# Four state scans on separate buffers, merged complex products, tables that start per base, shorter masks and a third parked query block in a fused attention and state-space kernel

## The chip, the cores and the metric

The kernel runs on one core of a Trainium2 chip. The metric is the device time of one launch in microseconds (us). Engines are named as in the profile: PE (TensorE matmul), PEld (its weight loads), DVE (VectorE), ACT (ScalarE), POOL (GpSimd), SP (SyncE, which issues nearly all DMAs).

## The reference

For x of shape 2048 x 512 in bf16, two branches are mixed by a gate:

```
g = sigmoid(sum(x * gate_w))                    # one number per row
a = softmax(q k^T / 4) v  for 32 heads of 16, q,k,v = x wqkv;   a = a wo
K[d,l] = Re( sum_n C[d,n] exp(dt[d] A[d,n] l) dt[d] B[d,n] )    # d < 512, n < 128, l < 2048
b = causal convolution of x with K along the rows, + x * Dskip
out = g * a + (1 - g) * b
```

Attention needs 32 x 2048 x 2048 exponentials. The convolution is done without an FFT, as a chunked state-space model: 32 chunks of 64 rows, a table of powers of the complex mode exp(dt A), states that are carried from chunk to chunk (the scan), and two small matmuls per chunk.

## The kernel before, in words

**Order of the work.** The kernel is written by a planner. Every instruction is an object `O` with an engine, the buffers it reads and writes, and a planned cost; `Prog.put` derives semaphore waits from them, also between two DVE instructions that depend on each other. Work is kept as threads (Python generators) with a priority; a smaller number goes first. `Sched.run` (line 363) takes, per exponential tile, the first thread in order of priority whose next instruction can start at once, and otherwise the least late one. A thread can wait for a flag (`("AFTER", name)`), for a tile number (`("Q", t)`) or for the one shared PSUM bank (`("LOCK", "MB")`); `landed` (line 326) gives the bank only when the planned landing of the transfers that its matmuls read lies 0.5 us back. The finished order is then fixed in each engine's instruction stream.

**Exponentials.** The scores are cut in 2048 slices of 512 columns, three to a tile; tiles go through two PSUM buffers SC. ACT takes the exponential of a tile in one instruction (line 755). From tile 380 on, `dchoose` (line 795) may give one slice of a tile to DVE, which makes it with integer and polynomial steps: line 767 for one slice, then four operations for a pair of slices (lines 787 to 791). Such slices use three PV matmuls each in place of one. `dchoose` returns without a choice when any DVE instruction of a thread with priority over 2.6 is ready, or when DVE is planned to be behind by more than a limit (4.6 or 5.5 us). Exponentials wait in rings: ET and EX, then EL (11 tiles, from tile 380) and EM (14 tiles, from tile 540). A block of 64 slices ends with a norm (lines 870 to 880).

**PE upkeep.** `lack` (line 246) counts planned PE activity in a window of 3.413 us; below NEED = 7.6 units the planner adds matmuls on a zero tile `wm`. Every matmul has an activity credit `u`, for example 0.05 for the gate's one-column matmuls.

**State-space half.** `params` (priority 10) computes the mode, its powers L1 to L48 and MU (the 64th) by `cmul` (line 904: four DVE operations, two of them 1024 wide in fp32) and one reciprocal (line 977). `bases` (11) makes four bases B16 of a quarter of the channels (128) each; `table` (9) makes eight pairs of blocks PT from them, after `base3` (line 1034). Each of the 16 blocks goes out to DRAM, comes back transposed as Qt, and meets the input blocks X2 in PE (`sstage`, line 1099: four PSUM evictions Sst a block); the chunk states go out and come back transposed into SG (`sload`, line 1124; three buffers for four quarters, so quarter 3 waits for `yq0`). `scan` (line 1142, priority 12) runs the quarters one after the other: 30 steps a quarter, each of five DVE operations on 128 channels, real and imaginary part: product with the real part of MU (s2), product with the imaginary part (s3), s2 plus SG, cast of the previous state into SG, and the sum into the state G. `ystage` (7.5) then makes 32 output units (line 1195), from Py and Tt loads, SG and X2; `yread`, `combine` and `outs` end the work.

**Start.** 14 one-column DVE operations (lines 661 to 669) make the two head masks; ACT first computes dt, then copies two parts of xT.

Of the kernel before, what the change touches and what calls it, by code (L numbers as in the profile page):

```python
# [6 lines left out]
FP32 = mybir.dt.float32  # L7
# [15 lines left out]
RS = 144  # L23
# [8 lines left out]
RINGS = ((24, "ET", NE), (380, "EL", 11), (540, "EM", 14))  # L32
DWS = ((380, 540 - 4, "DPL", "DCL", 4, 4.6), (540, 9999, "DPM", "DCM", 7, 5.5))
NEED = 7.6
# [3 lines left out]
SOLO = 1.0  # L38
ORDER = """
L8^ g1^ Q3^ VV^ VE ET D48 L4 EL CimT Dp^ fo^ OT^ nwi^ EX^ Qt^ Kst^ Q2^ Dpb Wv^ OnT2^ sgn u1^ X20^ sb_^ X23 gp^ Yl piota idf^ OnTp0  # L40
BimT Tt B161 Qp2^ L48^ SG0^ PT0 Q1^ B162 pt1 X22 SG1 OnT3^ BreT^ AreT ba^ cb^ MU SG2 OnT1 PT1 u4 L2 B163 g B160 Py^ dt^ wm L32 s3
an ON^ KT DPM ldt^ OnTp1^ xT^ ge^ AimT D16 Wk^ wrb^ X21^ tt2^ Sst hpi^ ft1^ Wq L16 ft2 zr tt1^ e2 idb^ EM VC^ x0n^ OnT0 Rz Q0 DPL
Yst^ u2 bn^ FP D32 DCM L1 CreT ea VL^ Wo Qp3^ msk s2^ DCL^ Qm^ gwT^ pt2 u3^ G zi
# [250 lines left out]
class Sched:  # L294
# [31 lines left out]
    def landed(self, ks):  # L326
        now = self.p.free["PE"] - .5
        return all(self.p.te[d] <= now for b, sl, *_ in (ks[0] if ks else ()) for d in b.st[sl][0].items())
# [80 lines left out]
def declare(nc, es):  # L409
# [9 lines left out]
    for k in (2, 3):  # L419
        sb(f"Qp{k}", 4 * 512)  # L420
# [65 lines left out]

    sb("SG0", 33 * 2 * RS)
    sb("SG1", 33 * 2 * RS)
    sb("SG2", 33 * 2 * RS)
    sb("G", 4 * 128, FP32)  # L490
    for n in ("s2", "s3"):
        sb(n, 2 * 128, FP32)

    for k in range(4):
        sb(f"X2{k}", 32 * 64)

# [11 lines left out]
    for n, free in (("ptd", NBLK * P * 2 * CB * T), ("sd", D * NCH * 2 * P),  # L508
                    ("kpd", NBLK * P * 8 * P), ("xrd", S * D), ("ytd", D * S), ("qd", 2 * P * 2048), ("od", 2 * P * S)):
# [66 lines left out]
def record(p, B, ins):  # L576
# [67 lines left out]
    for a in range(4):  # L644
# [9 lines left out]
        pool(lambda g: g.iota(pio(0, [[1, 1]]), [[0, 1]], base=0, channel_multiplier=1,  # L654
# [6 lines left out]
        dv(lambda v: v.memset(pio(1, [[1, 1]]), 0.0), [], [(pio, 1)], 1))  # L661
    for k in range(1, 8):
        put(dv(lambda v, k=k: v.scalar_tensor_tensor(pio(1 + k % 2, [[1, 1]]), pio(0, [[1, 1]]), 16.0 * k, pio(1 + (k - 1) % 2, [[1, 1]]),
                                                     ALU.is_ge, ALU.add), [(pio, 0), (pio, 1 + (k - 1) % 2)], [(pio, 1 + k % 2)], 1))
    put(dv(lambda v: v.memset(msk(0, [[1, 2]]), 0.0), [], [(msk, 0)], 1))
    for k in range(4):
# [939 lines left out]
```

## Time and profile before

| what | value |
|---|---|
| median of 6 runs (lowest, highest) | 881.92 us (877.23, 887.2) |
| the profiled execution, its span | 884.15 us, 882.4 us |
| mean granted PE clock | 0.986 |
| busy: PE, DVE, ACT | 786.5, 839.9, 859.6 us |
| exponential slices by DVE | 160 of 2048 |
| first exponential on ACT; end of the last | 13.3 us; 872.7 us |
| scan steps | 120, from 310 to 574 us |
| bytes by DMA | 96.5 MB |

A busy engine is not by itself the bound: the page gives averages over stages that are limited by different things, so the prediction reads busy time by stage, and the groups of instructions with their mean time. [...] two neighbours on DVE overlap by some 0.08 us, so what an instruction costs is read from the distance of starts in the timeline.

### The profile page before, as it was taken

The numbers are of one execution on the slowest core, as the hardware profiler recorded it, in microseconds if no ns is written. First come the engines' busy times: TensorE is split into PE (matmuls) and PEld (weight loads), VectorE is DVE, ScalarE is ACT, GpSimd is POOL, SyncE is SP. The second block draws the span as 40 slices with busy tenths as digits, with TensorE's granted clock in tenths as the row PEclk, the third lists the DMA queues.
The fourth block names the chain that finished last, engine by engine and source line by source line (L and its number), as shares of the span: only waits on it lengthen the run. The fifth ranks groups of instructions, "written<-read, shape, count | busy, mean of one in ns | idle before, by whom it ended". The sixth has DMA issues, their size and how long they took to land.

```text
span 882.4 us, 18472 instructions
## 1 busy us (share of the span) xinstructions
PE 786.5 (89%) x7566; PEld 248.3 (28%) x7566; DVE 839.9 (95%) x1802; ACT 859.6 (97%) x693; POOL 9.7 (1%) x18
## 2 busy tenths in 40 slices
PE   8988889998888888889899999999998998888887
PEld 3222222222222222222333334332332222222222
DVE  7999999999999999999999999999999999999992
ACT  7999999999999999999999999999999999999996
POOL 2000000000000000000000000000000000000000
PEclk9999999999999999998998899999999999999999
DMA  8410010006799999998866865545301100000000
GB/s 202 103 25 1 1 49 1 1 1 176 225 318 272 266 305 216 213 194 204 188 167 138 190 146 130 133 106 132 95 16 58 37 25 13 1 1 1 1 1 25
DMA packets 228564, 96.50 MB, mean 109 GB/s; under 512 B 192000, under 2 KB 215168, under 8 KB 226432
## 3 DMA queue, kind: packets, MB, share of 16 engines
q1 hardware_dynamic: 227280, 94.54, 43.8%
q8 instruction: 60, 0.98, 0.4%
q10 hardware_dynamic: 1200, 0.79, 0.4%
q14 instruction: 24, 0.20, 0.1%
HBM read 30.02 MB, written 37.75 MB: 77 GB/s over the span
## 4 chain that ended last, share of the span: by engine, by line
ACT 55%; DVE 35%; PE 6%; DMA 2%; issue 2%; ACTq 0%; DVEq 0%; SPq 0%
ACT ET L755 33%; ACT EL L755 15%; DVE EM L767 5%; DVE DCM L884 4%; ACT EM L755 4%; DVE ft L884 3%; ACT EX L755 3%; DVE tt L884 3%; PE OA L590 3%; DVE s L884 3%; PE SC L590 2%; DVE Sst L1113 2%; DVE EL L767 2%; DVE PT L884 1%; DVE DCL L884 1%
## 5 line engine op out<-in xcount | busy, mean ns | idle before, releaser
L755 ACT ACTIVATE ET<-SC 128x1536 bf16<-128x1536 f32 x362 | 488.5, 1655 | 5.6 <-PE SC L590 5.5
L590 PE MATMUL SC<-Qm,KT 32*128 32x512 bf16 x2048 | 269.9, 388 | 73.6 <-ACT ET L755 29.7
L590 PE MATMUL OA<-wm 128*128 128x512 bf16 x592 | 189.2, 395 | 1.8 <-DVE wm L656 1.0
L755 ACT ACTIVATE EL<-SC 128x1536 bf16<-128x1536 f32 (+1 forms) x160 | 183.7, 1351 | 0.6 <-PE SC L590 0.4
L590 PEld LDWEIGHTS SC<-Qm,KT 32*128 32x128 bf16 x2048 | 67.8, 91 | 335.3 <-ACT ET L755 162.2
L755 ACT ACTIVATE EM<-SC 128x1024 bf16<-128x1024 f32 (+1 forms) x143 | 157.1, 1246 | 1.7 <-PE SC L590 1.4
L590 PE MATMUL OA<-ET,VE 128*32 128x512 bf16 x1086 | 109.5, 398 | 0.7 <-DVE OT L872 0.7
L884 DVE TENSOR_TENSOR s<-G,MU 128x256 f32<-128x256 f32 x240 | 92.7, 419 | 3.3
L884 DVE TENSOR_TENSOR tt<-B,D 128x1024 bf16<-128x1024 bf16 x96 | 62.6, 682 | 0.5
L590 PEld LDWEIGHTS OA<-wm 128*128 128x128 bf16 x592 | 40.4, 98 | 76.5 <-issue 65.4
L767 DVE TENSOR_SCALAR EM<-SC 128x512 int16<-128x512 f32 x84 | 55.7, 679 | 0.5 <-PE SC L590 0.5
L767 DVE TENSOR_SCALAR EL<-SC 128x512 int16<-128x512 f32 x76 | 51.1, 682 | 1.8 <-PE SC L590 1.7
L884 DVE TENSOR_TENSOR G<-s,s 128x256 f32<-128x256 f32 x120 | 50.2, 418 | 0.1
L884 DVE TENSOR_TENSOR s<-s,SG 128x256 f32<-128x256 f32 x120 | 49.9, 416 | 0.0
L590 PE MATMUL OA<-EL,VE 128*32 128x512 bf16 x480 | 46.4, 389 | 0.0
L1113 DVE TENSOR_TENSOR Sst<-MB,sgn 128x512 bf16<-128x512 f32 x64 | 43.6, 682 | 1.9 <-PE MB L590 1.9
L590 PEld LDWEIGHTS OA<-ET,VE 128*32 128x32 bf16 x1086 | 27.6, 94 | 61.9 <-issue 59.7
L590 PE MATMUL OA<-EM,VE 128*32 128x512 bf16 x428 | 42.8, 390 | 0.1
L590 PE MATMUL MB<-Qt,X 64*32 64x256 bf16 x512 | 29.1, 303 | 9.5 <-DVE Sst L1113 5.8
L872 DVE STREAM_TRANSPOSE OT<-OA 128x512 f32<-128x512 f32 x32 | 22.7, 708 | 13.8 <-PE OA L590 13.8
L1155 DVE CAST SG<-G 128x256 bf16<-128x256 f32 x120 | 34.4, 287 | 0.1
L884 DVE TENSOR_TENSOR ft<-FP,L 128x1024 f32<-128x1024 f32 (+1 forms) x32 | 33.9, 1085 | 0.4
(163 smaller groups left out, 856.9 us busy)
## 6 DMA issues: line engine op xcount, KB each, us to landing
gm_ptd<-PT SPq DMA_DIRECT2D x16, 1024.0 KB, 6.2
Py<-gm_ptd SPq DMA_DIRECT2D x32, 512.0 KB, 4.6
gm_sd<-Sst SPq DMA_DIRECT2D x64, 128.0 KB, 2.8
gm_kpd<-Kst SPq DMA_DIRECT2D x16, 256.0 KB, 6.4
Tt<-gm_kpd SPq DMA_DIRECT2D x128, 32.0 KB, 3.6
gm_xrd<-in_A_x_dram SPq DMA_DIRECT2D x1, 2048.0 KB, 12.0
X<-gm_xrd SPq DMA_DIRECT2D x8, 256.0 KB, 5.2
gm_ytd<-Yst SPq DMA_DIRECT2D x32, 64.0 KB, 2.1
```

The source lines that it names most:

```text
L590: return O("PE", lambda t: t.matmul(out(), lhsT(), rhs(), start=start, stop=stop, skip_group_check=True, **kw), R, W, c, l, u)
L755: return ac(lambda a: a.activation(b(o, F), sc(0, F), AF.Exp, scale=LN2 / 128), [(sc, n, (t, n)) for n in ns], [et(t, n)[2] for n in ns], ...
L767: yield [dv(lambda v: v.tensor_scalar(b(o, [[1, 512]]).bitcast(I16), sc(512 * n, [[1, 512]]), -EOFF, EOFF, ALU.max, ALU.add), [(sc, n, (t, ...
L872: yield [dv(lambda v: v.transpose(OT(0, [[1, 512]]), OA(0, [[1, 512]])), [(OA, 0, b)], [(OT, 0, b)], 560)]
L884: return dv(lambda v: v.tensor_tensor(o(), a(), b_(), f), R, W, n, k)
L1113: yield [dv(lambda v, bank=bank: v.tensor_tensor(Sst(512 * bank, [[256, 2], [1, 256]]), MB(0, [[256, 2], [1, 256]]), sgn(0, [[0, 2], [1, 2 ...
L1155: return dv(lambda v: v.tensor_copy(sg(2 * RS * r, [[RS, 2], [1, 128]]), G(256 * (r % 2), V2)), [(G, r % 2)], [(sg, bl, (qr, 'G')) for bl ...
```

## The change

- The state scan becomes four threads (priority 12, 12.1, 12.2, 12.3), one for each quarter, each with its own SG, its own state G and its own products Gm. The two products of a step are one operation of 512 elements; MU is stored as imaginary part, real part, minus imaginary part for it.
- The loads of SG no longer wait for a freed buffer but for a tile number (172, 222, none, 300). Quarters 0 and 1 of X2 are loaded a second time into X2a and X2b for the y stage, after S13.
- Squares of complex numbers use `csq`, four operations of 512 elements. exp(-2 an) on ACT takes the place of a square and a reciprocal on DVE.
- `table` waits for the base that its pair of blocks needs (and one ahead), not for the last.
- `dchoose` ignores ready scan steps while the scan keeps to a straight line from its state at tile 380 to its end at tile 421. Ring EM has 13 tiles and starts at tile 548.
- The masks take three one-column operations. Query block 1 is stored and loaded back as blocks 2 and 3 are. One ACT copy of xT goes ahead of dt.
- `landed` asks for 2.5 us, NEED is 7.5, and the gate's matmuls have no activity credit. The order of placement in the on-chip memory is a new list.

```diff
-RINGS = ((24, "ET", NE), (380, "EL", 11), (540, "EM", 14))
-DWS = ((380, 540 - 4, "DPL", "DCL", 4, 4.6), (540, 9999, "DPM", "DCM", 7, 5.5))
-NEED = 7.6
+TL = 380
+TE = 548
+NL = 11
+NM = 13
+PEND1 = 4.6
+PEND2 = 5.5
+RINGS = ((24, "ET", NE), (TL, "EL", NL), (TE, "EM", NM))
+DWS = ((TL, TE - 4, "DPL", "DCL", 4, PEND1), (TE, 9999, "DPM", "DCM", 7, PEND2))
+NEED = 7.5
 WIN = 3.413
 HALF = .44
 TOL = .2
 SOLO = 1.0
+SGQ = (172, 222, 0, 300)
+SGP = 6
+SCN = 380, 421
...
     def landed(self, ks):
-        now = self.p.free["PE"] - .5
+        now = self.p.free["PE"] - 2.5
...
-    sb("SG0", 33 * 2 * RS)
-    sb("SG1", 33 * 2 * RS)
-    sb("SG2", 33 * 2 * RS)
-    sb("G", 4 * 128, FP32)
-    for n in ("s2", "s3"):
-        sb(n, 2 * 128, FP32)
+    for k, (a, b) in enumerate(PARTS):
+        sb(f"SG{k}", 33 * 2 * (128 * (b - a) + 16))
+    for k, (a, b) in enumerate(PARTS):
+        sb(f"G{k}", 512 * (b - a), FP32)
+        sb(f"Gm{k}", 512 * (b - a), FP32)
 
     for k in range(4):
+        sb(f"X2{k}", 32 * 64)
+    for k in "ab":
         sb(f"X2{k}", 32 * 64)
 
...
     put(dv(lambda v: v.memset(hpi(0, [[1, 1]]), HALF_PI), [], [(hpi, 0)], 1),
-        dv(lambda v: v.memset(pio(1, [[1, 1]]), 0.0), [], [(pio, 1)], 1))
-    for k in range(1, 8):
-        put(dv(lambda v, k=k: v.scalar_tensor_tensor(pio(1 + k % 2, [[1, 1]]), pio(0, [[1, 1]]), 16.0 * k, pio(1 + (k - 1) % 2, [[1, 1]]),
-                                                     ALU.is_ge, ALU.add), [(pio, 0), (pio, 1 + (k - 1) % 2)], [(pio, 1 + k % 2)], 1))
-    put(dv(lambda v: v.memset(msk(0, [[1, 2]]), 0.0), [], [(msk, 0)], 1))
-    for k in range(4):
-        put(dv(lambda v, k=k: v.scalar_tensor_tensor(msk(1, [[1, 1]]), pio(2, [[1, 1]]), 2.0 * k + 1, msk(1, [[1, 1]]),
-                                                     ALU.is_equal, ALU.add), [(pio, 2), (msk, 0)], [(msk, 0)], 1))
-    put(dv(lambda v: v.tensor_scalar(msk(0, [[1, 1]]), msk(1, [[1, 1]]), -1.0, 1.0, ALU.mult, ALU.add), [(msk, 0)], [(msk, 0)], 1))
+        dv(lambda v: v.tensor_scalar(pio(1, [[1, 1]]).bitcast(I32), pio(0, [[1, 1]]).bitcast(I32), 16, None, ALU.bitwise_and),
+           [(pio, 0)], [(pio, 1)], 1),
+        dv(lambda v: v.tensor_scalar(msk(1, [[1, 1]]), pio(1, [[1, 1]]).bitcast(I32), 1 / 16, None, ALU.mult), [(pio, 1)], [(msk, 0)], 1),
+        dv(lambda v: v.tensor_scalar(msk(0, [[1, 1]]), msk(1, [[1, 1]]), -1.0, 1.0, ALU.mult, ALU.add), [(msk, 0)], [(msk, 0)], 1))
...
-            if any(isinstance(x[3], list) and x[3][0].eng == "DVE" and (p.ready(x[3]) or 0) < end for x in sch.thr if x[0] > 2.6):
+            fore = scn[0] >= 120 - max(0, 120 - scn[1]) * (SCN[1] - t) / (SCN[1] - SCN[0])
+            if any(isinstance(x[3], list) and x[3][0].eng == "DVE" and (p.ready(x[3]) or 0) < end
+                   for x in sch.thr if x[0] > 2.6 and not (fore and x[0] >= 12)):
                 return
...
+
+    def csq(o, x, tk=("pt1", "pt2")):
+        o, x, t1, t2 = B[o], B[x], B[tk[0]], B[tk[1]]
+        k = int(o is B["MU"])
+        yield [tt(half(t1, 0), half(x, 0), half(x, 1), ALU.subtract, [(x, 0)], [(t1, 0)])]
+        yield [tt(half(t2, 0), half(x, 0), half(x, 1), ALU.add, [(x, 0)], [(t2, 0)])]
+        yield [dv(lambda v: v.scalar_tensor_tensor(o(D - D * k, [[1, D]]), x(0, [[1, D]]), 2.0, x(D, [[1, D]]), ALU.mult, ALU.mult),
+                  [(x, 0)], [(o, 0)], D)]
+        yield [tt(half(o, k), half(t1, 0), half(t2, 0), ALU.mult, [(t1, 0), (t2, 0)], [(o, 0)])]
+
+    def power(o, x, y):
+        return csq(o, x) if x == y else cmul(o, x, y)
...
         for o, x, y in (("L2", "L1", "L1"), ("L4", "L2", "L2"), ("L8", "L4", "L4")):
-            yield from cmul(o, x, y)
+            yield from power(o, x, y)
...
-        yield [tt(perm("u1"), nat("ea"), nat("ea"), ALU.mult, key("ea"), key("u1"))]
-        yield [dv(lambda v: v.reciprocal(B["e2"](0, [[1, D]]), B["u1"](0, [[1, D]])), key("u1"), key("e2"), 3050)]
+        yield [ac(lambda a: a.activation(B["e2"](0, PERM), B["an"](0, NAT), AF.Exp, scale=-2.0), key("an"), key("e2"), D)]
...
-        yield [dv(lambda v: v.tensor_scalar(MU(2 * D, [[1, D]]), MU(D, [[1, D]]), -1.0, None, ALU.mult), key("MU"), [(MU, 1)], D, 2)]
+        yield [dv(lambda v: v.tensor_scalar(MU(2 * D, [[1, D]]), MU(0, [[1, D]]), -1.0, None, ALU.mult), key("MU"), [(MU, 1)], D, 2)]
...
         yield ("AFTER", "projs")
         yield ("AFTER", "gate")
-        yield ("AFTER", "base3")
         t1, t2 = B["tt1"], B["tt2"]
         for pb in range(NBLK // 2):
             qr, blks = pb // 2, (2 * pb, 2 * pb + 1)
             PT = PTs[pb % 2]
+            yield ("AFTER", f"base{min((pb + 1) // 2, 3)}")
...
+    XY = [B["X2a"], B["X2b"], X2[2], X2[3]]
...
     def sload(blk):
-        qr, bl = divmod(blk, 4)
-        if qr == 3:
-            yield ("AFTER", "yq0")
-        elif qr == 1:
-            yield ("AFTER", "sgfree")
-            yield ("Q", p.q + 3)
-        sg = SG[qr % 3]
+        k, sg, rs, a = part(blk // 4)
+        bl = blk - 4 * a
+        yield ("Q", max(SGQ[k], p.q + 3))
         if bl == 0:
-            yield [pool(lambda g: g.memset(sg(0, [[1, 2 * RS]]), 0.0), [], [(sg, "z")], 256)]
-            if qr < 3:
-                yield [pool(lambda g: g.memset(sg(2 * RS + 128, [[RS, 64], [1, 16]]), 0.0), [], [(sg, "pad")], 1024)]
-        yield [dma("SP", lambda e: e.dma_start_transpose(sg(2 * RS + CB * bl, [[RS, 64], [1, CB]]),
+            yield [pool(lambda g: g.memset(sg(0, [[1, 2 * rs]]), 0.0), [], [(sg, "z")], 2 * rs)]
+        yield [dma("SP", lambda e: e.dma_start_transpose(sg(2 * rs + CB * bl, [[rs, 64], [1, CB]]),
                                                          sd.dram(CB * blk * 8192, [[8192, CB], [1, 8192]])),
-                   [(sd, (blk, i)) for i in range(4)], [(sg, bl, (qr, 'S'))], 6.3, 2.6)]
+                   [(sd, (blk, i)) for i in range(4)], [(sg, bl, (k, 'S'))], 6.3, 2.6)]
         sch.mark(f"sg{blk}")
...
-        def quarter(qr):
-            sg, d0 = SG[qr % 3], 128 * qr
...
+        def run(k):
+            G, Gm = B[f"G{k}"], B[f"Gm{k}"]
+            a, b = PARTS[k]
+            sg, rs, d0, w, nb = SG[k], 128 * (b - a) + 16, 128 * a, 128 * (b - a), 4 * (b - a)
+            V2 = [[w, 2], [1, w]]
+            ks = [(sg, bl, (k, 'S')) for bl in range(nb)]
...
             for r in range(2, NCH):
-                k, o = r % 2, 1 - r % 2
-                yield [tt(lambda o=o: s2(0, V2), lambda o=o: G(256 * o, V2), lambda: MU(d0, [[0, 2], [1, 128]]), ALU.mult,
-                          [(G, o), (MU, 0)], [(s2, 0)], 256)]
-                yield [tt(lambda: s3(0, V2), lambda o=o: G(256 * o + 128, [[-128, 2], [1, 128]]), lambda: MU(D + d0, [[D, 2], [1, 128]]), ALU.mult,
-                          [(G, o), (MU, 0), (MU, 1)], [(s3, 0)], 256)]
-                yield [tt(lambda: s2(0, V2), lambda: s2(0, V2), lambda r=r: sg(2 * RS * r, [[RS, 2], [1, 128]]), ALU.add,
-                          [(s2, 0)] + ks, [(s2, 0)], 256)]
+                o, i = r % 2, 1 - r % 2
+                yield [tt(lambda: Gm(0, [[2 * w, 2], [w, 2], [1, w]]), lambda i=i: G(2 * w * i + w, [[-w, 2], [0, 2], [1, w]]),
+                          lambda: MU(d0, [[D, 2], [D, 2], [1, w]]), ALU.mult, [(G, i), (MU, 0), (MU, 1)], [(Gm, 0), (Gm, 1)], 4 * w)]
+                yield [tt(lambda: Gm(0, V2), lambda: Gm(0, V2), lambda r=r: sg(2 * rs * r, [[rs, 2], [1, w]]), ALU.add,
+                          [(Gm, 0)] + ks, [(Gm, 0)], 2 * w)]
                 if r > 2:
                     yield [cast(r - 1)]
-                yield [tt(lambda k=k: G(256 * k, F), lambda: s2(0, F), lambda: s3(0, F), ALU.add, [(s2, 0), (s3, 0)], [(G, k)], 256)]
+                yield [tt(lambda o=o: G(2 * w * o, V2), lambda: Gm(0, V2), lambda: Gm(2 * w, V2), ALU.add, [(Gm, 0), (Gm, 1)], [(G, o)], 2 * w)]
+                scn[0] += b - a
+                if p.q <= SCN[0]:
+                    scn[1] = scn[0]
             yield [cast(NCH - 1, True)]
-            sch.mark(f"scan{qr}")
+            for qr in range(a, b):
+                sch.mark(f"scan{qr}")
 
         yield ("AFTER", "scanpar")
-        for qr in range(4):
-            yield from quarter(qr)
+        for k in range(len(PARTS)):
+            sch.add(run(k), 12 + .1 * k)
...
             yield ("AFTER", f"scan{qr}")
             yield ("AFTER", f"yl{u}")
+            while 1 not in XY[qr].st:
+                yield ("Q", p.q + 1)
             yield ("LOCK", "MB", [(Py, r)] + [(Tt, (r, par, a)) for par in range(2) for a in range(2)])
...
         for qr in range(4):
-            yield ("Q", 30) if qr == 0 else ("AFTER", f"S{4 * qr - 3}")
-            for par in range(2):
-                yield [dma("SP", lambda e, qr=qr, par=par: e.dma_start(X2[qr](0, [[64, 32], [1, 64]], 64 * par, 64),
-                                                                       B["xrd"].dram(64 * qr + 256 * par, [[32 * D, 64], [D, 32], [1, 64]])),
-                           [(B["xrd"], 0)], [(X2[qr], par)], 8, 1.9)]
+            yield ("Q", 30) if qr == 0 else ("AFTER", f"S{4 * qr - 2}")
+            yield from fetch(X2[qr], qr)
             sch.mark(f"ub{qr}")
+        yield ("AFTER", "S13")
+        for qr in range(2):
+            yield from fetch(XY[qr], qr)
...
-                      [xk(lt // 4, q4), (gwT, 0)], [(MB, 0, 'gate')], q4 == 0, q4 == 3, c=.06, l=.2, u=.05)
+                      [xk(lt // 4, q4), (gwT, 0)], [(MB, 0, 'gate')], q4 == 0, q4 == 3, c=.06, l=.2, u=0.0)
...
-        for c, q in ((2, 322), (3, 458)):
+        for c, q in ((1, 156), (2, 322), (3, 458)):
...
-    put(copy_dve(*cp[0]), copy_dve(*cp[2]))
+    put(copy_dve(*cp[0]), copy_dve(*cp[2]), copy_act(*cp[1]))
     put(O("ACT", lambda a: a.activation(B["dt"](0, [[1, D]]), B["ldt"](0, [[1, D]]), AF.Exp), key("ldt"), key("dt"), .55))
-    put(copy_act(*cp[1]), copy_act(*cp[3]))
+    put(copy_act(*cp[3]))
```

## The prediction

> **What bounds the kernel now.** I read the page first, then busy time by stage, then the groups with shapes kept apart, then the DVE timeline inside the scan. Engine totals:
>
> ```profile
> PE 786.5 (89%) x7566; PEld 248.3 (28%) x7566; DVE 839.9 (95%) x1802; ACT 859.6 (97%) x693; POOL 9.7 (1%) x18
> ```
>
> ACT is full, and DVE is full beside it. They share one pool of work: 2048 exponential slices of 512 columns, of which DVE took 160 (76 into EL, 84 into EM). So DVE time is worth something: what it does not spend on the state-space half, it can spend on exponentials. The stage table (us; PE, PEld, DVE, ACT busy with counts, then PE clock, DMA share, GB/s) and the same stretches for the DVE exponential, line 767, alone:
>
> ```profile
> 531.00:576.00 45.00, 43.61 (x620) 17.21 (x619) 42.99 (x131) 45.00 (x35) 0.00 (x0) 1.00 0.57 139
> 576.00:720.00 144.00, 131.49 (x1406) 42.74 (x1406) 142.06 (x291) 143.38 (x132) 0.00 (x0) 1.00 0.27 67
> 720.00:860.00 140.00, 120.84 (x1012) 34.11 (x1009) 139.40 (x280) 138.30 (x129) 0.00 (x0) 0.99 0.02 5
> ```
>
> ```profile
> 440.00:531.00 91.00, 0.00 (x0) 0.94 0.69 158
> 531.00:576.00 45.00, 0.69 (x1) 1.00 0.57 139
> 576.00:720.00 144.00, 52.44 (x78) 1.00 0.27 67
> 720.00:860.00 140.00, 53.70 (x81) 0.99 0.02 5
> ```
>
> No slice goes to DVE before 531 us, where tile 380 and ring EL begin, and one from 531 to 576: there DVE is busy with the rest of the scan. The last scan cast stands at 573.7 us; from then on 159 slices follow in 284 us. The scan itself, from the DVE timeline (start, duration; an "x2" covers two):
>
> ```profile
> 499.54 0.76 DVE L884 TENSOR_TENSOR s<-G,MU 128x256 f32<-128x256 f32 x2
> 500.21 0.42 DVE L884 TENSOR_TENSOR s<-s,SG 128x256 f32<-128x256 f32 x1
> 500.55 0.29 DVE L1155 CAST SG<-G 128x256 bf16<-128x256 f32 x1
> 500.75 0.42 DVE L884 TENSOR_TENSOR G<-s,s 128x256 f32<-128x256 f32 x1
> 501.20 0.76 DVE L884 TENSOR_TENSOR s<-G,MU 128x256 f32<-128x256 f32 x2
> ```
>
> One step recurs every 1.66 us (499.54 to 501.20). Independent 256-wide operations start 0.33 us apart and the cast takes 0.20, so five operations make 4 x 0.333 + 0.20 = 1.53; the other 0.12 to 0.13 is the next product waiting for the sum written just before it.
>
> Last, stretches of 4 us with a low PE clock:
>
> ```profile
> 408.00:412.00 4.00, 4.00 (x32) 0.84 (x24) 3.46 (x9) 2.96 (x3) 0.00 (x0) 0.56 0.62 117
> 412.00:416.00 4.00, 4.00 (x38) 1.07 (x35) 2.82 (x8) 3.17 (x4) 0.00 (x0) 0.58 1.21 294
> 480.00:484.00 4.00, 4.00 (x46) 1.27 (x38) 3.96 (x14) 2.96 (x3) 0.00 (x0) 0.52 0.60 121
> 484.00:488.00 4.00, 4.00 (x41) 1.12 (x40) 2.58 (x8) 3.37 (x3) 0.00 (x0) 0.50 1.15 269
> 488.00:492.00 4.00, 4.00 (x23) 0.86 (x22) 3.93 (x13) 2.97 (x3) 0.00 (x0) 0.70 0.95 168
> ```
>
> ACT loses 1.04 + 0.83 = 1.87 us at 408 to 416, where PE stood waiting for a Qt transfer (1.4 us in the waits), and 1.04 + 0.63 + 1.03 = 2.70 us at 480 to 492, inside the y stage. Two more dips, at 132 (the gate's 64 one-column matmuls) and 784 us, cost 0.29 and 0.88.
>
> [...] 419 ns at 256 elements, 682 to 688 at 512, 1218 at 1024, about 1.04 ns per element. [...] Here 0.333 us minus 267 ns gives 66 ns: that is what one instruction less is worth. [...]
>
> **The exchange rate.** From 720 to 860 us DVE is busy 139.4 us; six norms (0.64 + 0.15 + 0.34 + 0.27 + 0.31 = 1.71 us each by their starts) and four output evictions (0.67) take 13. So (139.4 - 13) / 81 = 1.56 us of DVE per slice. What a slice takes from ACT is the difference of two rows:
>
> ```profile
> L755 ACT ACTIVATE EM<-SC 128x1024 bf16<-128x1024 f32 x85 | 81.5, 1082 | 0.7 <-PE SC L590 0.6
> L755 ACT ACTIVATE EM<-SC 128x1536 bf16<-128x1536 f32 x58 | 81.1, 1488 | 1.0 <-PE SC L590 0.8
> ```
>
> 81.1/58 = 1.40 and 81.5/85 = 0.96, so 0.43 us. If DVE is freed by d and takes n slices more, the span falls by 0.43 n, and DVE loses that time too: d = (1.56 + 0.43) n. One us freed gives 0.50 slice and 0.216 us of span. By the same argument one us of ACT time removed or added changes the span by 1 - 0.216 = 0.78 us.
>
> **The change part by part.**
>
> *Merged scan product.* Two 256-wide products (2 x 0.333) become one of 512 (0.600, as the other 512-wide fp32 rows start): 0.067 x 120 steps = 8.0 us of DVE.
>
> *Interleaving.* A lone new step is 0.600 + 0.333 + 0.20 + 0.333 = 1.47, plus two exposed dependences of 0.12 (product to add, sum to next product; the cast still covers the third) = 1.71, worse than 1.66. With a second quarter on its own G and Gm every gap is filled: 1.47. Before, from 320 to 530 us, the listed DVE operations sum by starts to 195 of 210 us, idle stalls are some 5, so 10 us of gaps remain for 96 steps: 0.105 per step. Full cover is worth 0.105 x 120 = 12.6 us. Quarters have equal claims only by order: two alternate at a time, and quarter 0 starts alone from tile 172 (244 us), when tables fill its gaps. I take 12.6; bounds 0 and 14.
>
> *Squares.* The rows of a complex product and the reciprocal:
>
> ```profile
> L884 DVE TENSOR_TENSOR pt<-L 128x1024 f32<-128x1024 f32 x12 | 14.3, 1218 | 0.1
> ...
> L884 DVE TENSOR_TENSOR L<-pt,pt 128x512 f32<-128x512 f32 x12 | 8.1, 672 | 0.1
> ...
> L977 DVE RECIPROCAL e<-u 128x512 f32<-128x512 f32 x1 | 3.3, 3344 | 0.0
> ```
>
> Six squares lose two 1024-wide products (1.13 by starts) for two 512-wide ones: 2 x 0.53 = 1.07, and one exposed wait, 0.12: 1.19 x 6 = 7.1 us. L48, VL stay products.
>
> *Reciprocal.* 3.25 by starts, and the ea square 0.60: 3.85 us off DVE. ACT gets one 512-column exp; its like (ea, line 1404) lasts 0.64, by slope 0.43 to 0.5: ACT +0.5, span +0.4. No table load, since it is Exp amid Exp.
>
> *Tables per base.* The same instructions sooner: the table may start after base 0 instead of base 3 at 192 us, some 45 us earlier. DVE is 98% busy there anyway, so nothing falls on the path; the DMA phase (share 1.01 from 300 to 380) starts while the queue is idle, and bases fill the tables' 0.12 us gaps. Some 160 such gaps stand in bases and tables, partly filled now: worth 0 to 10, I take 3 us.
>
> *Exponentials beside the scan.* The choice of a slice no longer yields to a ready scan step once the scan keeps its pace. It removes the hole at the switch (DVE idle 2.0 us in 560 to 580). The freed time must find slices at tile 380: what the scan did after 531 us was 43 us of DVE, so up to about 43 us freed can be absorbed. Bound: beyond that DVE would idle before tile 380.
>
> *Landing margin 0.5 to 2.5 us, gate counted as no activity.* Both aim at dips above: ACT 1.87 + 0.29 = 2.16, span 1.7. Behind a wrongly early S matmul stood the score matmuls, hence ACT. The y dip (2.70) has another cause and stays. NEED 7.5 for 7.6 removes some warm matmuls; they lie in PE's slack, 14% from 720 on, so nothing gained; see the rival.
>
> *Three-operation masks, ACT copy first.* The masks ended at 6.0 us, ahead of x0n at 6.3: nothing. The copy fills ACT's wait for ldt; an started at 8.10 because DVE was busy, so dt 0.2 later is covered: within 0.2 either way.
>
> *DMAs and queues.* Added: one store and one load of Q1 (0.5 MB each), four X loads of 0.25 MB (one seen issue held SP for 3 us, another 0.5; 5.2 us to land), fewer POOL memsets. About 2 MB on 96.5. They pass on SP ahead of Py, Tt and Yst transfers; in 440 to 531 the DMA share is 0.69. The y stage now also waits for the new X buffers after S13; before, its 32 evictions ran from about 437 to 665 us and the first outputs went out at 700, the last exp at 872, so 100 us late would still be hidden.
>
> Sum: 8.0 + 12.6 + 7.1 + 3.85 + 3 + 2 = 36.5 us of DVE, so 18 slices (178) and 7.9 us of span; plus 0.4, minus 1.7: -9.2 us. The profiled execution was 884.15 us, its span 882.4: 873.2 and about 875. It lies 2.2 above the median of 881.92 (runs 877.23 to 887.2), so for the median I take 872.7.
>
> **The rivals.**
>
> *A wider gain.* The y dips go too (DMA spread out, later locks): 2.70 + 0.88 times 0.78 = 2.8; all base and table gaps fill: 7 us more DVE, 1.5. That gives 868.4. For: DMA shares of 0.6 to 1.15 stand in the stretches of the dips. Against: 784 us has no DMA.
>
> *The interleaving finds no partner.* Quarters gated by their loads (quarter 3 not before tile 300, about 417 us) run alone at 1.71: scan 120 x 0.05 = 6 us dearer instead of 20.6 cheaper. DVE freed 7.1 + 3.85 + 2 - 6 = 7, span 1.5; with +0.4 and -1.7 this is -2.8: 879. Against it: before, all 16 S blocks were done at 438 us, so two quarters should be there together.
>
> *The clock gives way: slower.* The plan holds PE activity just over NEED; [...] The four dips cost ACT 5.74 us, 1.43 each, 1.1 of span. Eight more dips eat the gain; sixteen make 891. [...] For: 1.3% less margin. Against: the dips seen had causes of their own (a wait, one-column matmuls), not a bare margin.
>
> **How the numbers follow.** First case 0.55 (own range 869 to 877), wider gain 0.22, no partner 0.14, clock 0.09. One per cent, about what a measurement of this kernel tells from none, is 873.1. The first case lies at that border, and most of what I left out (gaps in bases and tables) is gain: 0.35 of it counts as faster, 0.20 as same. Faster 0.35 + 0.22 = 0.57; same 0.20 + 0.14 = 0.34; slower 0.09. Range 865 to 881: it takes in the wider gain with some slices more, and the no-partner case.
>
> **What would show it.** Right: 170 to 186 slices at line 767's operation, some between 531 and 576; products of 128x512 at about 688 ns, 120 of them; steps of two quarters alternating with starts 0.33 and 0.60 apart; ACT busy 7 us less; no clock dip at 132 and 410. Wrong: DVE idle between 480 and 531 (nothing to do before tile 380), 160 slices again, new dips, or outputs after the last exp.

## The result, and the profile after

The changed kernel takes 880.2 us (median of 32 runs, 875.26 to 882.81) against 883.74 us for the kernel before on the same chips (67 runs): a ratio of 0.9956, 95% interval 0.9942 to 0.9969. That is 3.5 us less; 9.2 were forecast. The profiled execution has a span of 878.6 us (before 882.4). Its time, 880.42 us, is near the median; its mean clock, 0.982, is below the 0.9875 that the 32 runs have on average.

The line of engine totals of the page after, to set beside the first fence of the prediction:

```profile
PE 780.5 (89%) x7548; PEld 246.4 (28%) x7548; DVE 835.1 (95%) x1717; ACT 854.0 (97%) x694; POOL 6.4 (1%) x15
```

ACT is 5.6 us less busy. But span minus ACT busy, that is ACT's idle time, rose from 882.4 - 859.6 = 22.8 to 878.6 - 854.0 = 24.6 us. The slices on DVE (stage table of the DVE exponential, now line 774; columns us, DVE busy with count, clock, DMA share, GB/s):

```profile
440.00:531.00 91.00, 0.00 (x0) 1.00 0.60 148
531.00:576.00 45.00, 13.27 (x20) 1.00 0.56 127
576.00:720.00 144.00, 50.49 (x76) 1.00 0.21 50
720.00:860.00 140.00, 53.10 (x80) 0.99 0.02 5
```

176 slices instead of 160, and 20 of them where there was one: the freed DVE time was found and spent as the prediction said. The scan's and the tables' groups (out<-in, shapes, count, busy us, mean ns, idle before):

```profile
L893 DVE TENSOR_TENSOR Gm<-G,MU 128x512 f32<-128x512 f32 x120 | 80.9, 684 | 1.2
...
L893 DVE TENSOR_TENSOR Gm<-Gm,SG 128x256 f32<-128x256 f32 x120 | 49.3, 417 | 0.9
...
L893 DVE TENSOR_TENSOR pt<-L 128x512 f32<-128x512 f32 x12 | 7.8, 686 | 0.1
...
L998 ACT ACTIVATE e<-an 128x512 f32<-128x512 f32 x1 | 1.2, 1172 | 0.0
```

The 120 merged products last 684 ns, the squares' first operations 686 ns instead of 1218. The last row is the ACT exponential that took the reciprocal's place.

What went wrong shows in 4-us stretches with a low PE clock (us; PE, PEld, DVE, ACT, POOL busy; clock; DMA share; GB/s):

```profile
288.00:292.00 4.00, 4.00 (x25) 0.85 (x24) 3.71 (x8) 3.06 (x3) 0.00 (x0) 0.50 0.98 353
292.00:296.00 4.00, 4.00 (x32) 0.98 (x31) 2.39 (x6) 3.19 (x3) 0.00 (x0) 0.50 0.74 148
...
416.00:420.00 4.00, 0.42 (x8) 0.20 (x8) 1.37 (x3) 1.54 (x2) 0.00 (x0) 0.71 1.03 239
420.00:424.00 4.00, 4.00 (x33) 0.89 (x25) 3.13 (x8) 2.58 (x2) 0.00 (x0) 0.50 0.78 209
```

The dips of before at 132, 410 and 480 us are gone, but between 288 and 296 us ACT loses 0.94 + 0.81 us, and between 416 and 424 us 2.46 + 1.42. A third new dip stands at 372 to 380. The DVE timeline there (start, duration, [idle before <- releaser]) and the waits from 410 to 421 us (total, times, longest):

```profile
414.94 0.42 DVE L893 TENSOR_TENSOR G<-Gm 128x256 f32<-128x256 f32 x1
418.63 0.29 DVE L1174 CAST G<-SG 128x256 f32<-128x256 bf16 x1 [3.27 <-DMA SG<-gm_sd]
418.84 0.68 DVE L1135 TENSOR_TENSOR Sst<-MB,sgn 128x512 bf16<-128x512 f32 x1
```

```profile
PE MB L601 <- DVE Sst L1135: 4.0, 1, 4.0
ACT ET L762 <- PE SC L601: 3.3, 1, 3.3
DVE G L1174 <- DMA SG<-gm_sd: 3.3, 1, 3.3
```

Read them as a chain. DVE reached the first step of the third quarter's scan, the cast of its first state row (line 1174), at 415.4 us, and stood 3.27 us because the SG load had not landed. Queued behind it on DVE was an eviction of a state block (Sst, line 1135); PE needed its PSUM bank and stood 4.0 us; the score matmuls behind that on PE came late, so ACT stood 3.3 us. From 417.7 us the clock is 0.50 for 6.8 us (in the first dip for 13.6, from 284.6), and ACT loses a fifth to a third of its time there as well (0.81 to 1.42 us of 4). At 279 us the first quarter's cast waited 1.28 us in the same way. By the planner's own times the cast of the third quarter was due at 409.74 us and the load at 409.69: ordered with 0.05 us to spare; the four quarters of the change have 1.0, 1.0, 0.05 and 9.0 us. In the kernel before, by the same planner, a quarter's first cast came 1.0 us after its last load in the first quarter and 13 to 19 us after it in the others.

### The profile page after: what moved, and what is told of

Same layout as the page of the kernel before. It is cut to its first block, busy times and chain, and to the rows that moved or that the text cites. A ratio compares the mean times of both kernels' runs of the same rounds, so it can differ in the third digit from the quotient of the medians.

```text
span 878.6 us, 18380 instructions
## 1 busy us (share of the span) xinstructions
PE 780.5 (89%) x7548; PEld 246.4 (28%) x7548; DVE 835.1 (95%) x1717; ACT 854.0 (97%) x694; POOL 6.4 (1%) x15
## 4 chain that ended last, share of the span: by engine, by line
DVE 46%; ACT 43%; PE 6%; issue 2%; DMA 2%; ACTq 0%; DVEq 0%; SPq 0%
ACT ET L762 29%; DVE Gm L893 10%; ACT EL L762 9%; DVE EM L774 5%; DVE DCM L893 5%; DVE G L893 4%; DVE EL L774 3%; ACT EX L762 3%; PE OA L601 3%; DVE DCL L893 3%; PE SC L601 2%; DVE SG L1177 2%; ACT EM L762 2%; DVE Sst L1135 2%; PE MB L601 2%
## 5 line engine op out<-in xcount | busy, mean ns | idle before, releaser
L762 ACT ACTIVATE EL<-SC 128x1024 bf16<-128x1024 f32 (+1 forms) x168 | 186.4, 1287 | 0.9 <-PE SC L601 0.4
L601 PE MATMUL OA<-wm 128*128 128x512 bf16 x547 | 177.1, 397 | 1.8 <-DVE wm L667 1.0
L762 ACT ACTIVATE EM<-SC 128x1024 bf16<-128x1024 f32 (+1 forms) x135 | 147.9, 1262 | 0.3
L893 DVE TENSOR_TENSOR Gm<-G,MU 128x512 f32<-128x512 f32 x120 | 80.9, 684 | 1.2
L774 DVE TENSOR_SCALAR EL<-SC 128x512 int16<-128x512 f32 x96 | 63.8, 679 | 1.3 <-PE SC L601 1.2
L601 PEld LDWEIGHTS OA<-wm 128*128 128x128 bf16 x547 | 37.9, 98 | 73.0 <-issue 62.4
L774 DVE TENSOR_SCALAR EM<-SC 128x512 int16<-128x512 f32 x80 | 53.1, 678 | 0.0
L893 DVE TENSOR_TENSOR Gm<-Gm,SG 128x256 f32<-128x256 f32 x120 | 49.3, 417 | 0.9
L893 DVE TENSOR_TENSOR G<-Gm 128x256 f32<-128x256 f32 x120 | 49.2, 417 | 0.0
L601 PE MATMUL MB<-Qt,X 64*32 64x256 bf16 x512 | 30.3, 314 | 10.8 <-DVE Sst L1135 8.5
L601 PE MATMUL OA<-EM,VE 128*32 128x512 bf16 x404 | 38.9, 391 | 0.1
L881 DVE STREAM_TRANSPOSE OT<-OA 128x512 f32<-128x512 f32 x32 | 22.7, 709 | 13.6 <-PE OA L601 13.6
L893 DVE TENSOR_TENSOR ft<-FP,L 128x1024 f32<-128x1024 f32 (+1 forms) x32 | 34.4, 1084 | 0.1
## 6 DMA issues: line engine op xcount, KB each, us to landing
gm_xrd<-in_A_x_dram SPq DMA_DIRECT2D x1, 2048.0 KB, 12.1
```

The costliest lines, as they stand in the source:

```text
L601: return O("PE", lambda t: t.matmul(out(), lhsT(), rhs(), start=start, stop=stop, skip_group_check=True, **kw), R, W, c, l, u)
L762: return ac(lambda a: a.activation(b(o, F), sc(0, F), AF.Exp, scale=LN2 / 128), [(sc, n, (t, n)) for n in ns], [et(t, n)[2] for n in ns], ...
L774: yield [dv(lambda v: v.tensor_scalar(b(o, [[1, 512]]).bitcast(I16), sc(512 * n, [[1, 512]]), -EOFF, EOFF, ALU.max, ALU.add), [(sc, n, (t, ...
L881: yield [dv(lambda v: v.transpose(OT(0, [[1, 512]]), OA(0, [[1, 512]])), [(OA, 0, b)], [(OT, 0, b)], 560)]
L893: return dv(lambda v: v.tensor_tensor(o(), a(), b_(), f), R, W, n, k)
```

## The experiments

Ratios are to the kernel before, run on the same chip. "ACT idle" is ACT's idle time from 24 to 860 us, added up over 2-us windows of one profile: 7.9 before, 10.8 in the change. Every variant is planned anew and has its own list of placements; how far its order differs from that of the change is said where it matters. Each idle time is that of one execution, and executions of one kernel differ by several us: the profile of e3 took 5.2 us more than e3's median, that of e7 5.6 more, that of e4 4.1 less. Less that distance the three idle 11.4, 11.9 and 12.1 us, so differences of a few us between single idle times tell nothing.

**The first step of each scan later.** e1 adds one line ahead of the cast:

```diff
                 yield ("AFTER", f"sg{4 * a + bl}")
+            yield ("Q", p.q + 12)
```

> Edit: the first instruction of each quarter scan (the cast of the first state from SG into G on DVE) is planned 12 tiles after the SG load is issued, not at its planned landing; 174 slices for DVE instead of 176. Theory of the early cast: DVE no longer stands at that cast (1.28 and 3.27 us in the changed kernel), so no half clock at 284 to 300 and 416 to 428 us, ACT idle about 8 us less, less 0.9 for two slices: ratio to before 0.986 to 0.991. Rival, PE activity too thin with NEED 7.5: the low clock stays in those stretches, ratio 0.994 to 0.998. Rival, the dips are chance: other dips in other places, ratio as the changed kernel, 0.9956.

Measured: 0.9945 (0.9922 to 0.9968), 879.48 us. No cast waited for SG and the stretches at 284 and 416 were gone, yet ACT idle was 9.3. The waits from 326 to 337 us show what came instead:

```profile
PE MB L602 <- DVE Sst L1136: 3.1, 3, 1.8
DVE Sst L1136 <- DMA gm_sd<-Sst: 1.8, 2, 1.2
...
ACT ET L763 <- PE SC L602: 1.4, 2, 1.1
```

Now DVE stands before Sst, because the store of an earlier block (gm_sd<-Sst) had not yet read the buffer. The wait was removed, most of its cost was not: the gain of 0.5 to 1% on the change that the theory of the early cast expected did not come.

**NEED back to 7.6.** e2: `NEED = 7.5` to `NEED = 7.6`.

> Edit: NEED back to 7.6, all else as changed, 176 slices; the casts of the first state stand at the same place in the plan. Theory of the early cast: both waits (about 1.3 and 3.3 us) and both dips of the clock are there again, ratio to before 0.994 to 0.998. Rival, thin activity: the dips at 284 and 372 us are gone and the ratio is 0.986 to 0.991.

Measured: 0.9985 (0.997 to 1.0), just above the range of the first theory; the dips at 284 and 416 stood as in the change. It is a weak test of the rival of the clock: up to 535 us of the plan (the planner's own times) the order comes out the same as in the change, on every engine, so the stretches with the dips were run by the same program; over the whole kernel there are 583 matmuls on `wm`, against 588 in the change.

**One scan after another.** e3:

```diff
-            sch.add(run(k), 12 + .1 * k)
+            yield from run(k)
```

> Edit: the four scans run one after the other on their own buffers, all else as changed; 168 slices. What the interleaving is worth: by the prediction 12.6 us of DVE, 2.7 us of span; by slices 8 x 0.43 = 3.4 us. A lone step should recur every 1.71 us. Theory of the early cast: quarter 2's cast comes long after its load, so the 3.3 us wait and its dip vanish (worth some 3.5 us of span), quarter 0's wait of 1.3 us stays: the two cancel, ratio to before 0.994 to 0.998, with ACT busy 3.4 us more and ACT idle 4 us less. Rival, thin activity: no change of the dips, ratio 0.998 to 1.001.

Measured: 1.0012 (0.9996 to 1.0027), 168 slices, ACT busy 857.6, ACT idle 16.6, of which 11.7 from 220 to 440 us. The wait of the third quarter's cast went, as expected, but ACT's idle time did not fall, and the ratio lies above both ranges: DVE now waited 5.1 us for Sst stores. So interleaving is worth 8 slices, 3.6 us of ACT; the two times differ by 4.9 us, of which another order alone could make a part (below).

**No slices pulled ahead of ready scan steps.** e4: `fore = False and scn[0] >= ...`.

> Edit: the choice of a slice for DVE again yields to any ready scan step, all else as changed; 174 slices. By the exchange rate two slices are 0.9 us: ratio to before 0.995 to 0.998, and no slice for DVE while a scan is ready, as before. The theory of the early cast expects both waits and dips to stay, since the casts stand where they stood; the rival, that the dips come from chance, expects them elsewhere.

Measured: 0.9978 (0.9962 to 0.9994), 174 slices, ACT busy 854.0, as in the change. This part is worth two slices; the 0.2% between e4 and the change are no more than other orders make (below). Up to 525 us of the plan the order is that of the change, too, so e4 does not test this part's share in the waits before that.

**Three more ways round the late load.** e5 puts the cast on GpSimd, planned at 3.7 us; e6 is e1 and e4 together; e7 plans the SG loads 3 us and the Sst stores 1.5 us later:

```diff
-            yield [dv(lambda v: v.tensor_copy(G(2 * w, V2), sg(2 * rs, [[rs, 2], [1, w]])), ks, [(G, 1)], 2 * w, 2)]
+            yield [pool(lambda g: g.tensor_copy(G(2 * w, V2), sg(2 * rs, [[rs, 2], [1, w]])), ks, [(G, 1)], 4000)]
...
-"SG": (2.7, 2.5, 3.0)
+"SG": (2.7, 2.5, 6.0)
-"sd": (.45, .5, 2.1)
+"sd": (.45, .5, 3.6)
```

> The changed kernel with the first step of each quarter scan (the cast of its first state row to float32) on GpSimd instead of VectorE, planned there at 3.7 us, so that a late SG load holds up GpSimd, which has nothing else queued, and VectorE reaches the scan's first product some 3 us later than the load's planned landing. 176 slices, as in the change. Theory late landings (what the change lost are the half-clock stretches that begin where VectorE waits for an SG load): no wait of VectorE for SG, ScalarE's idle time between 24 and 860 us falls from 10.8 to 7 us or less, ratio to the kernel before 0.989 to 0.992. Rival moving stretches (the stretches belong to the order as a whole and come back elsewhere): ratio 0.993 to 0.997, ScalarE idle 9 us or more, with other waits at their start.

> Undoes one part of the change (no slices on D operands pulled in while a scan's step is ready, as in e4_no_fore) and puts each scan's first step 12 exponentials later (as in e1_seed_late); 176 slices. In e4_no_fore the one long stretch left was the one at the SG load at 414 us. Theory late landings: with that wait away ScalarE idles 4 us or less between 24 and 860 us, ratio 0.987 to 0.991. Rival moving stretches: 0.993 to 0.998, as e1_seed_late and e4_no_fore each gave.

> The changed kernel, ordered with later landings: the SG loads are planned 3 us later and the Sst stores 1.5 us later than in the change, so that everything behind them is ordered later; 174 slices. Theory late landings: VectorE waits for DMA less than 1 us between 220 and 560 us (5.3 in the change, 3.9 on Sst in e1_seed_late), ScalarE idle 7 us or less, ratio 0.988 to 0.992. Rival moving stretches: 0.993 to 0.997 with VectorE's waits for DMA still 3 us or more, or gone and other waits in their place.

Measured: e5 0.9984 (0.9967 to 1.0002), ACT idle 12.1; e6 0.9938 (0.9916 to 0.9961), 9.9; e7 1.0004 (0.9984 to 1.0024), 17.6. In none did DVE wait for an SG load, and in all three it waited 2.0 to 3.4 us for Sst stores. Only e6 lies in the range of a theory, that of the moving stretches; e5 and e7 came out slower than either expected. In e7 4.6 us more were a wait of an unrelated buffer (OnTp) for a transfer out of PT, whose place it had been given: that is the placement's doing, and e7 tells little. The late SG load is a real wait, but removing it alone gained 0.2% at most (e1, e6).

**The squares alone.** e8: the kernel before with `csq` and the ACT exponential only.

> The kernel before with the squares of the tables in four operations instead of four longer ones and the reciprocal replaced by one exponential on ScalarE; nothing of the scans or the gate. 11 us of VectorE work less; the order takes up 4 slices more (164). By the prediction's exchange rate 4 slices are 1.7 us less on ScalarE, less 0.4 for the exponential: ratio 0.998 to 0.999. If all of the 11 us had turned into span at 0.216: 0.997. Rival, the freed time lies where no slice can use it: 1.000 to 1.002.

Measured: 1.0072 (1.0046 to 1.0099), a miss on every side. 164 slices, ACT busy 0.5 us less, but ACT idle 13.0, of which 7.2 between 300 and 380 us. There DVE waited 4.4 us for Sst stores, though this kernel has none of the new SG loads, the added transfers of X2 and of query block 1, or the larger landing margin. A new order of the kernel before had cost more than four slices bring. That raised a question: was the order of before unusually good?

**Other orders of both kernels.** Each pair changes one constant of the planner by so little that the work stays nearly the same (e15 has two slices fewer) and only ties fall the other way: EXP 0.0633 to 0.0635 (e9, e11), the landing of Tt loads 2.7 to 2.8 (e10, e12), LAT 0.055 to 0.054 (e13, e15), the landing of Qt loads 3.7 to 3.9 (e14, e16).

> The kernel before with one constant of its planner changed by 0.2 ns (EXP 0.0633 to 0.0635, the planned fixed part of an exponential). The work is the same, 160 slices, and the planner's own end moves by 0.6 us to the good side, but from the first tie that falls the other way the order of the queues is another. Theory favourable order (before's order was chosen among many with few late landings; any new order costs some us of waits at landings, so the change was set against a kernel that another order wouldn't have matched): ratio 1.004 to 1.009, ScalarE idle 10 us or more between 24 and 860 us (7.9 before). Rival, the change itself brings the waits (four scans, SG loads, earlier D slices): 0.998 to 1.002, ScalarE idle within 1.5 us of before's.

> The kernel before with one constant of its planner changed by 0.1 us (planned landing of a Tt load 2.7 to 2.8). Same work, 160 slices, planner's end 0.7 us earlier, another order of the queues. Theory favourable order: ratio 1.004 to 1.009, ScalarE idle 10 us or more between 24 and 860 us. Rival, the change itself brings the waits: 0.998 to 1.002.

> The changed kernel with the same 0.2 ns as e9_before_exp: same work, 176 slices, planner's end 0.5 us later, another order. Theory favourable order: against e9_before_exp, the same constant on the other kernel, the change is worth 0.7 to 1.2%; against the kernel before the ratio is anywhere from 0.992 to 0.999. Rival, the change itself brings the waits: 0.994 to 0.998, and no more than 0.5% better than e9_before_exp.

> The changed kernel with the same 0.1 us on Tt loads as e10_before_tt: same work, 176 slices, planner's end 0.1 us later. Theory favourable order: 0.7 to 1.2% better than e10_before_tt. Rival, the change itself brings the waits: 0.994 to 0.998, and no more than 0.5% better than e10_before_tt.

> The kernel before with the planner's LAT 0.055 changed to 0.054 us; same work, 160 slices, planner's end 0.7 us earlier, another order from about a third of the program on. Two other orders of the kernel before gave 1.0085 and 1.0021. Theory favourable order: the mean over orders of the kernel before lies at 1.003 to 1.006, so this one between 1.001 and 1.009. Rival (before's order is an ordinary one): 0.997 to 1.001.

> The kernel before with the planned landing of a Qt load 0.2 us later (3.7 to 3.9); same work, 160 slices, planner's end 0.7 us earlier, another order. Theory favourable order: 1.001 to 1.009. Rival: 0.997 to 1.001.

> The changed kernel with the same LAT as e13_before_latm; 174 slices, planner's end 1.2 us later. Theory favourable order: 0.6 to 1.2% better than e13_before_latm, and 0.993 to 0.999 against the kernel before. Rival: no more than 0.5% better than e13_before_latm.

> The changed kernel with the same Qt landing as e14_before_qt; 176 slices, planner's end the same, only a few steps of VectorE and some of TensorE in another place. Theory favourable order: 0.6 to 1.2% better than e14_before_qt, 0.993 to 0.998 against the kernel before. Rival: no more than 0.5% better than e14_before_qt.

| constant | before: ratio (interval) | ACT busy, idle | change: ratio (interval) | ACT busy, idle |
|---|---|---|---|---|
| as it is | 1 | 859.6, 7.9 | 0.9956 (0.9942-0.9969) | 854.0, 10.8 |
| EXP | 1.0085 (1.0053-1.0117) | 860.5, 10.6 | 0.9961 (0.9942-0.9979) | 853.2, 8.4 |
| Tt | 1.0021 (1.0006-1.0036) | 860.6, 7.4 | 0.9964 (0.995-0.9979) | 853.3, 8.8 |
| LAT | 0.9982 (0.9965-0.9998) | 860.4, 9.3 | 1.0031 (1.0017-1.0046) | 854.5, 15.8 |
| Qt | 1.001 (0.999-1.0031) | 860.5, 6.4 | 0.993 (0.9903-0.9958) | 852.9, 11.8 |
| mean | 1.0020 | 860.3, 8.3 | 0.9968 | 853.6, 11.1 |

The theory of a favourable order is not borne out: the order of before is 0.2% better than the mean of its like, within their scatter (standard deviation 0.4% for either kernel). Pair by pair it is split: the EXP pair (1.2%) and the Qt pair (0.8%) gave the gain that the theory wanted or more, the LAT pair a loss of 0.5%, the Tt pair 0.57%, between the two. Averaged over orders the change is worth 0.51%, with a standard error of 0.24% from the two scatters, so the forecast 1.05% stands two errors away, and so does no gain at all. The error is rather larger than that, since the orders are not independent: the DVE timelines of before and its Tt order are the same for 503 us, those of the change and its Tt order for 467 us, and the change plans the scans' first casts within 0.06 us of the same times in four of its five orders.

ACT busy is the same within 1.6 us in all orders of one kernel; ACT idle is not. Where the mean idle time differs is plain: between 220 and 440 us it is 3.9 us over the five orders of before and 9.2 over those of the change; elsewhere the change has 2.5 less. In all five orders of the change DVE stands before the casts that read SG, 3.1 to 6.3 us in all, and goes on within 0.2 us of a load's landing (the profile puts 2.6 to 4.5 us of it down to the load); in the orders of before it stands 0.4 us at most for a load. The waits of e16 from 370 to 420 us are the same chain again:

```profile
PE MB L602 <- DVE Sst L1136: 4.4, 1, 4.4
DVE G L1175 <- DMA SG<-gm_sd: 4.2, 1, 4.2
...
ACT ET L763 <- PE SC L602: 3.7, 1, 3.7
```

The slowest order of the change, e15, also has a wait of the kind that was set aside in e7. Its OnTp is placed over PT, and DVE stood there until 310.6 us, when a transfer out of PT landed:

```profile
310.61 0.71 DVE L889 STREAM_TRANSPOSE OnTp<-ON 128x512 bf16<-128x512 bf16 x1 [2.57 <-issue]
```

The profile names no releaser for it. Without e15 the four other orders would put the change at 0.67%.

**The tables at their old place.** e17 and, in a second order (the Qt constant), e18:

```diff
         yield ("AFTER", "gate")
+        yield ("AFTER", "base3")
...
-            yield ("AFTER", f"base{min((pb + 1) // 2, 3)}")
```

> Undoes one part of the change: the tables wait for the third base again, as in the kernel before; all else as in the change. 168 slices, so ScalarE some 3.4 us busier than in the change. Theory crowding (the earlier tables, S blocks and scans meet the transfers at DMA share 1 between 220 and 440 us, and that is where the idle time of the changed kernel comes from, whatever the order): ScalarE idle between 220 and 440 us falls from a mean of 9 over five orders of the change to 5 or less (3.9 over five orders of the kernel before); ratio to the kernel before 0.995 to 0.999. Rival (the idle time comes with the four scans and the loads they need): idle 8 us or more there, ratio 0.999 to 1.004.

> A second order of e17_base3, with the planned landing of a Qt load 0.2 us later, as in e14_before_qt and e16_after_qt; 172 slices. Theory crowding: ScalarE idle 5 us or less between 220 and 440 us, ratio 0.994 to 0.998. Rival: 8 us or more, 0.998 to 1.004.

Measured: e17 0.9999 (0.9983 to 1.0015), 168 slices, ACT busy 856.1, ACT idle 12.3 from 220 to 440 us; e18 1.0058 (1.004 to 1.0075), 172 slices, 856.2, and 8.1 there with 4.6 more up to 531. In e17 6.2 us of it are again a wait that the placement brought (Gm for a transfer out of PT). Less that, some 6 is left, between the two theories; e18 has no such wait and still 8.1. By its ratio e17 falls to the rival, and e18 is slower than either expected. So the idle time does not go with the early tables alone, and undoing them costs 2 to 3 us of ACT time.

## Why the prediction was wrong, step by step

**The exchange rate held.** In the profiled pair ACT is busy 5.6 us less for 16 slices, the new exponential (1.2 us) included, so a slice took (5.6 + 1.2) / 16 = 0.42 us from ACT; over five orders, with 15.6 slices more in the mean, (6.7 + 1.2) / 15.6 = 0.51. Forecast 0.43.

**The DVE terms nearly held in sum, not singly.** The gaps between dependent operations can be added up from the DVE timeline: start to next start, less the duration minus 0.085 us (independent operations overlap by that), less the stalls that are listed. From 300 to 578 us they are 15.6 us before, 9.4 in the change and 23.4 in e3. Interleaving therefore saves 14 us against a lone new scan, but only 6.2 against before, where I took 12.6 (full cover): for much of the first two quarters one scan runs alone, and there a step shows two exposed waits. The change at 321 us, one scan, and at 472 us, two:

```profile
321.90 0.42 DVE L893 TENSOR_TENSOR G<-Gm 128x256 f32<-128x256 f32 x1
322.35 0.69 DVE L893 TENSOR_TENSOR Gm<-G,MU 128x512 f32<-128x512 f32 x1
323.08 0.42 DVE L893 TENSOR_TENSOR Gm<-Gm,SG 128x256 f32<-128x256 f32 x1
```

```profile
472.59 0.68 DVE L893 TENSOR_TENSOR Gm<-G,MU 128x512 f32<-128x512 f32 x1
473.19 0.42 DVE L893 TENSOR_TENSOR G<-Gm 128x256 f32<-128x256 f32 x1
473.53 0.42 DVE L893 TENSOR_TENSOR Gm<-Gm,SG 128x256 f32<-128x256 f32 x1
473.86 0.28 DVE L1177 CAST SG<-G 128x256 bf16<-128x256 f32 x1
```

Alone, the product starts 0.45 us after the sum it reads, where 0.33 is the spacing, and the sum of products 0.73 after the product, where 0.60 is. With two scans the starts are 0.33 to 0.34 and 0.60 apart. From 24 to 300 us the gaps fell from 13.2 to 7.1 us: 6.1, mostly in bases and tables, where I took 3. The hole at the switch went (stalls from 440 to 578 us: 3.8 before, none after). Merged products 8.0 (independent f32 operations start 0.333 us apart at 256 elements and 0.60 at 512, so one for two saves some 0.067, 8.0 over 120 steps) and squares, 6.4 without the waits that the gaps hold already, are as costed, by rows that last what I took (684 and 686 ns at 512 elements). With 6.2 for 12.6, 6.1 for 3 and 3.8 for 2 the sum is 8.0 + 6.2 + 6.4 + 3.85 + 6.1 + 3.8 = 34.4 us of DVE; less the new waits for DMA, 5.4 against 0.2 us from 220 to 560, it is 29.2, and 29.2 / 1.99 is 15 slices: 16 were taken. The sum came near the forecast 36.5 by luck: a term half as large as forecast was made up by two that were twice as large.

**The steps that failed** are the term "*Landing margin 0.5 to 2.5 us ... ACT 2.16, span 1.7*", which is all that was forecast for ACT's idle time, and behind it a term that was put at nothing: that DVE would stand waiting for a transfer ("*so nothing falls on the path*", said of the early tables). The dips that I named did go in the profiled pair, those at 132 and 410 us, and the y dip at 480 with them (in e16 one stands at 131 us again); new dips, which the prediction names as a sign of being wrong, stand in their place. But ACT's idle time from 24 to 860 us did not fall by 2.16 us; it rose by 2.8 in the mean over orders (2.9 in the profiled pair). Worked through for the profiled pair: -9.2, plus 0.9 for two slices fewer, plus 4.6 for 2.9 in place of -1.7, plus 0.7 for an exponential of 1.17 us in place of 0.5, less 1.0 at the start (below), is -4.0; the spans differ by -3.8. So the idle time is by far the largest part of the miss. I had asked of each transfer whether the queues could carry it, and not who waits for it and what is queued behind the waiter. The margin of 2.5 us guards only the PSUM bank of a matmul; the DVE cast that opens a scan has none. In before three of the four scans were late enough that their loads had long landed; once DVE had time for a scan at the very moment of landing, DVE met its DMAs, at SG or, with that moved, at the Sst stores. The chain from the SG load to ACT is shown; that it is the cause of all the idle time is not, since e1, e5 and e6 took it away and had 9.3 to 12.1 us left.

**The start.** ACT copies first: "within 0.2 either way". ACT idles 5.5 us in the first 24 us over five orders of the change, 6.5 over those of before: 1.0 us gained.

**The rivals.** Wider gain: the y dip and the gaps of bases and tables did go, and their gain was eaten by the same waits. No partner: half right, for the first two quarters. Clock gives way: this needed eight more dips in an execution. Over five orders each, before shows 12 stretches of low clock between 24 and 860 us and the change 15, and in the profiled pair each stretch of the change that cost ACT over 0.1 us stands at a stop of PE of 1.0 us or more. So dips without a stop are not what was lost; e2 tells no more, since its order there is that of the change. That a planned activity of 7.5 units in place of 7.6 lowers the clock was my assumption; no run shows it.

**What stays open.** Which part brings the waits to 220 to 440 us. Not the interleaving alone (e3 has 11.7 us of ACT idle there), not the early tables alone (e17, e18). The early slices and NEED were not tested there, since e4 and e2 leave the order before 525 us as it is. What all these share, own SG buffers loaded by tile number, more transfers, and the larger landing margin, was not tried apart; that e8, without any of these, waits for Sst stores as well says that they are not needed for such a loss.

## What to carry to other kernels

A planned order that is tight to the landing of a transfer can become a wait (here 0.05 us of plan became 3.27 us of DVE, 4.0 of PE and 3.3 of ACT): for each operation whose input becomes ready just as its engine becomes free, look at what is queued behind it on that engine and price a miss of a few us. Here freeing DVE moved its work closer to its loads, in the plan from 13 to 19 us down to 0.05 to 9 for three of the four first casts, and moving that one wait moved the loss to the next transfer (Sst stores, 3.9 us of DVE in e1). And where the order comes from a planner, compare several orders of both versions: one constant changed by 0.2 ns, with the placement that came with it, moved the kernel before by 0.85%. Look also at where two orders part: a variant whose order parts from the first only behind the stretch in question is the same program there, and tests nothing about it.

## What the runs showed of the hardware

In the twenty profiles, between 24 and 860 us, all 23 stops of PE of 1.6 us or more (up to 6.2) came with a stretch of clock 0.50 that held them or began within 4 us after them, 3.4 to 20.5 us long; of the 41 stops of 1.0 to 1.6 us, 24 did and 17 did not. Over 59 runs of the kernel before (those beside e9 to e12) a mean clock lower by 0.01 went with a span longer by 3.7 us. The exponential on ACT with an output order of every second element (128x512 float32) took 1.16 to 1.17 us in all fifteen profiles that have it, its like with the output in order 0.63 to 0.64. It brought no table load to ACT: in both profiles of the pair there are three, of 1.28 us each, all ahead of 13.4 us: before the first instruction, before the sine and before the exponential that follows it.
